# A fused attention and gated-MLP kernel on one core: x of tiles 2 and 3 loads earlier, V of three tiles is open at once, and ACT makes four more roots

## The chip, the core and the metric

The kernel runs on one NeuronCore of a Trainium2 chip. Five engines each work through their own list of instructions and wait for one another by semaphores: TensorE (PE: matrix products and transposes, written to PSUM), VectorE (DVE), ScalarE (ACT), GpSimd (POOL) and SyncE (SP), which issues all the transfers of this kernel in one queue. Weight loads of PE have a row of their own (PEld). The metric is device time in microseconds (us), less is better.

## The reference

Two branches share one layer norm over 2048 tokens of width 640: linear attention with 32 heads of width 20 and a softmax feature map, and a gated MLP of width 1536.

```python
x = A_x
xn = _layernorm(x, axis=-1)
return x + _A_ref(xn, A_wqkv, A_w_phi, A_wo) + _B_ref(xn, B_w1, B_w3, B_w2)

# _A_ref
qkv = (x @ wqkv).reshape(B, S, 3, H, Dh).transpose(2, 0, 3, 1, 4)
pq = jnp.einsum("bhsd,hdf->bhsf", q, w_phi)
pk = jnp.einsum("bhsd,hdf->bhsf", k, w_phi)
phi_q = jnp.concatenate([_softmax(pq), _softmax(-pq)], axis=-1)
phi_k = jnp.concatenate([_softmax(pk), _softmax(-pk)], axis=-1)
kv = jnp.einsum("bhsf,bhsd->bhfd", phi_k, v)
z  = jnp.einsum("bhsf->bhf", phi_k)
num = jnp.einsum("bhqf,bhfd->bhqd", phi_q, kv)
den = jnp.einsum("bhqf,bhf->bhq", phi_q, z)[..., None] + 1e-6
o = num / den          # then @ wo

# _B_ref
h = _silu(x @ w1) * (x @ w3)
out = h @ w2
```

## The kernel before

Tokens are cut into 16 tiles of 128; a column of the gated MLP's hidden layer is a unit of 128 columns by 512 tokens. The order of all instructions is written out by hand (`manual_schedule`): each engine runs its instructions in the order of the Python text, so a line moved in the text is moved in the queue of its engine, and SP's transfers go out in the order of their `ld` and `by_dma` calls. PSUM has eight banks: six come from the pool `bank`, two from `pair`. A tile taken from the pool gets a bank whose earlier tile is done with, and its first product waits for that tile's last reader.

The change lies in the first 25 us. Needed there:

- **Loads** (L163 to L178, L751, L778 to L831). `ld_tiles(t, n)` loads x of n tiles, `ld_wv(c, 1)` one row (128 of the 640 inputs) of V's weights, 160 KB each, like one tile of x. `ld_glu1` and `ld_glu` load pieces of 256 columns of w1 and w3.
- **Layer norm.** `ln_stats` (DVE, L245 and L248) makes mean and variance of a tile. For tiles 0 to 3 `ln_root` (ACT, L263) makes the standard deviation and a DVE reciprocal (L728, in `lx`) its inverse `rstd`. For the other tiles `stats` has POOL do it, with a power and a Newton step (`ln_pow`, `ln_newton`). `ln_x` (DVE, L287) normalises x in place. `BY_DMA = 4` is the bound between the two ways.
- **Transposes.** Products need x with the width on the partitions. `by_pe(dst, t)` makes five PE transposes (L305) into one bank `pst` and two ACT copies (L309) out of it. `by_dma(t)` has SP's queue transpose a tile (L751). Of normalised x (`xnT`), tiles 0, 1 and 3 go by PE and the others by DMA.
- **Raw V.** So that V of tiles 0 to 3 need not wait for the norm, it is made of x as loaded: `by_pe(xrT, t)`, then `raw_part(t, c, ps)` for the five weight rows c (two products, 360 and 280 columns, L316). `raw_scaled` (ACT, L327) multiplies with `rstd` on the way out of PSUM; the mean's share is taken off much later.
- **First gated units.** `glu_half(i, w, sc, fi, ps)` (L478) makes one half, 256 tokens, of the gate (w1) or the up product (w3): half 0 needs tiles 0 and 1, half 1 tiles 2 and 3. Eight halves make the first two units; their banks are ga, ua, gb, ub. Then follow whole units (`unit`, L461: g2, g3) and V of the other tiles (`V(4)` on, L359). A unit is finished by tanh (ACT, L472, after a table load at L813, since the roots use another table) and two DVE products (L489, L492), which free its banks. In the text `g0 = glu_done(...)` issues tanh and `g0()` the two DVE products.

Before, raw V is done in two pairs: tiles 0 and 1 row by row as the weight rows land, then tile 2, then tile 3.

Of the kernel before, what the change touches and what calls it, by code (L numbers as in the profile page):

```python
# [8 lines left out]
P = 128  # L9
# [3 lines left out]
def kernel(  # L13
# [17 lines left out]
    nc = tc.nc  # L31
    bf = mybir.dt.bfloat16
# [9 lines left out]
    HD = D // 2  # L42
    EPS = 1e-5
    SAFE = 36.0
    BY_DMA = 4
    WARM = 20
    RAW = 4

# [18 lines left out]
    def bank(name, dt=f32):  # L67
        n = 512 if dt == f32 else 1024
        return psum.tile([P, n], dt, name=name, tag="bank")
# [86 lines left out]
    with tc.manual_schedule():  # L156
# [6 lines left out]
        def ld_tiles(t, n):  # L163
            ld(
                xin[:, (t // 4) % 3, t % 4 : t % 4 + n],
                x2[t * P : (t + n) * P, :].rearrange("(t p) d -> p t d", p=P),
            )
# [4 lines left out]

        ld_tiles(0, 1)
        ld_tiles(1, 1)
        for c in range(KD):
            ld_wv(c, 1)
        ld_tiles(2, 1)
        ld_tiles(3, 1)  # L178


        ident = one.tile([P, P], bf, name="ident")
# [57 lines left out]
        def ln_stats(*ts):  # L239
            made = []  # L240
            for t in ts:
                xt = xin[:, (t // 4) % 3, t % 4, :]
                st = work.tile([P, 2, 6], f32, name="st")
                for i in range(2):
                    nc.vector.bn_stats(out=st[:, i, :], in_=xt[:, i * HD : (i + 1) * HD])  # L245
                made.append(st)
            for t, st in zip(ts, made):
                nc.vector.bn_aggr(out=mv[:, t, :], in_=st[:])  # L248
# [40 lines left out]
                op0=ALU.subtract, op1=ALU.mult,  # L289
            )  # L290

        def x_transposed(*ts):

            for t in ts:
                xn = xin[:, (t // 4) % 3, t % 4, :]
                if t >= BY_DMA:
                    nc.sync.dma_start_transpose(out=xnT[:, :, t * P : (t + 1) * P], in_=xn)
                    continue
                by_pe(xnT, t)

        def by_pe(dst, t):
            xt = xin[:, (t // 4) % 3, t % 4, :]
            ps = bank("pst", bf)
            for c in range(KD):
                nc.tensor.transpose(  # L305
                    ps[:, c * P : (c + 1) * P], xt[:, c * P : (c + 1) * P], ident[:]
                )
            for c0, c1 in ((0, 2), (2, KD)):
                nc.scalar.copy(  # L309
                    out=dst[:, c0:c1, t * P : (t + 1) * P],  # L310
                    in_=ps[:, c0 * P : c1 * P].rearrange("p (c s) -> p c s", s=P),
                )

        def raw_part(t, c, ps):
            for i, (a, b) in enumerate(((0, CH), (CH, D))):
                nc.tensor.matmul(  # L316
                    ps[i][:, 0 : b - a],
                    xrT[:, c, t * P : (t + 1) * P],
                    wv[:, c, a:b],
                    start=(c == 0),  # L320
                    stop=(c == KD - 1),
                    skip_group_check=True,
                )

        def raw_scaled(t, ps):
            for i, (a, b) in enumerate(((0, CH), (CH, D))):
                nc.scalar.activation(  # L327
                    out=v_raw[:, t, a:b], in_=ps[i][:, 0 : b - a],
                    func=AF.Identity, scale=rstd[:, t : t + 1],
                )  # L330
# [390 lines left out]
        def stats(t0, n):  # L721
            ln_stats(*range(t0, t0 + n))
            ln_pow(t0, n)
            ln_newton(t0, n)

        def lx(t0, n):
            if t0 < BY_DMA:
                nc.vector.reciprocal(out=rstd[:, t0 : t0 + n], in_=ry[:, t0 : t0 + n])  # L728
            for t in range(t0, t0 + n):
                ln_x(t)  # L730

        T = x_transposed

        def unit(banks=None):
            return glu_unit(*glu.pop(0), banks)
# [1 line left out]
        def two(name):  # L739
            both = pair(name)  # L740
            return both[:, 0], both[:, 1]
# [11 lines left out]
        def ld_glu1(w, src, f0, f1):  # L753
            ld(w[:, :, f0:f1], src[:, f0:f1].rearrange("(c p) f -> p c f", p=P))

        by_pe(xrT, 0)
        warm(4)
        ln_stats(0)
        ln_root(0)
        by_pe(xrT, 1)  # L760
        ln_stats(1)
        ln_root(1)
        vps = [two("v0"), [bank("pv"), bank("pv")]]
        lx(0, 1)
        for c in range(2):
            raw_part(0, c, vps[0])
            raw_part(1, c, vps[1])
        T(0)
        raw_part(0, 2, vps[0])
        raw_part(1, 2, vps[1])  # L770
        lx(1, 1)
        T(1)
        raw_part(0, 3, vps[0])
        raw_part(1, 3, vps[1])
        raw_part(0, 4, vps[0])
        by_pe(xrT, 2)
        raw_part(1, 4, vps[1])
        ld_glu1(w1, B_w1, 0, 256)  # L778
        nc.gpsimd.tensor_copy(out=xin[0:1, 1, 0, 0:1], in_=ry[0:1, 1:2])
        ld_tiles(4, 2)  # L780
# [1 line left out]
        ld_tiles(6, 2)  # L782
        ln_stats(2)
        ln_root(2)
        by_pe(xrT, 3)
        ln_stats(3)
        ln_root(3)
        lx(2, 1)
        by_dma(2)
        ld_glu(256, 512)  # L790
        ld_tiles(8, 2)
        ld_tiles(10, 2)
        raw_scaled(0, vps[0])
        lx(3, 1)
        raw_scaled(1, vps[1])
        ps2 = [bank("pv"), bank("pv")]
        for c in range(KD):
            raw_part(2, c, ps2)
        ps3 = [bank("pv"), bank("pv")]
        for c in range(KD):  # L800
            raw_part(3, c, ps3)
        (sc, fa), (_, fb) = glu.pop(0), glu.pop(0)
        ga, ua = two("g0")
        glu_half(0, w1, sc, fa, ga)
        T(3)
        raw_scaled(2, ps2)
        raw_scaled(3, ps3)
        gb = bank("gp")[:]
        glu_half(0, w1, sc, fb, gb)
        glu_half(0, w3, sc, fa, ua)  # L810
# [1 line left out]
        glu_half(0, w3, sc, fb, ub)  # L812
        nc.scalar.activation(out=table[:], in_=nought[:, 0:1], func=AF.Tanh)  # L813
        nc.gpsimd.tensor_mul(out=drift[:], in0=mv[:, 0:RAW, 0], in1=rstd[:, 0:RAW])
        stats(4, 2)
        stats(6, 2)
        glu_half(1, w1, sc, fa, ga)
        glu_half(1, w3, sc, fa, ua)
        glu_half(1, w1, sc, fb, gb)
        glu_half(1, w3, sc, fb, ub)  # L820
        g0 = glu_done(sc, fa, ga, ua)
        g1 = glu_done(sc, fb, gb, ub)
        lx(4, 2)
        by_dma(4)
        by_dma(5)
        ld_tiles(12, 2)
        g0()
        g2 = unit()
        lx(6, 2)
        by_dma(6)  # L830
        by_dma(7)  # L831
        ld_tiles(14, 2)
# [155 lines left out]

    with tc.If(ok == 0):
        nc.gpsimd.memset(v_one[:, :, 0], 1.0)  # L990
        for i in range(7):
            nc.gpsimd.memset(state[:, 93 * i : 93 * (i + 1)], 0.0)
        halves = [state[:, 0 : 6 * VC], state[:, 6 * VC :]]
        with tc.For_i(0, NST, 1) as t:
            cols = bass.ds(t * P, P)
            v_unit(v_one, cols)
            phi_unit(0, wkphi, "pk", exps_less_max, cols)
            acc = pair("pkv")
            kv_unit(0, v_one, acc, True, True)
            for i, half in enumerate(halves):  # L1000
                n = half.shape[1]
                nc.vector.tensor_tensor(out=half, in0=half, in1=acc[:, i, 0:n], op=ALU.add)
        kv_done(halves)
        with tc.For_i(0, NST, 1) as t:
# [36 lines left out]
```

## Time and profile before

| what | us |
|---|---|
| median of 3 runs (267.69 to 268.8) | 268.13 |
| the profiled execution, its own time | 268.32 |
| its span, first instruction to last | 266.6 |
| busy: PE | 260.7 (98%) |
| busy: DVE | 194.3 (73%) |
| busy: ACT | 114.2 (43%) |
| busy: POOL | 91.1 (34%) |

The first 24.3 us of the profiled execution, by stretch (busy us of each engine, granted PE clock, share of the 16 DMA engines):

| stretch | PE | DVE | ACT | POOL | clock | DMA |
|---|---|---|---|---|---|---|
| 0 to 4.6 | 3.68 | 1.57 | 2.15 | 3.17 | 1.00 | 0.54 |
| 4.6 to 8.5 | 3.55 | 1.69 | 2.62 | 0.18 | 1.00 | 0.83 |
| 8.5 to 12.1 | 3.60 | 3.31 | 3.12 | 0.20 | 1.00 | 1.00 |
| 12.1 to 17.2 | 4.94 | 4.05 | 4.50 | 2.74 | 1.00 | 0.88 |
| 17.2 to 24.3 | 7.04 | 6.48 | 2.84 | 1.92 | 1.00 | 1.10 |

How to read it: times inside the profile count from the span's start. A busy share says how much of a stretch an engine had an instruction under way; a product's row includes the latency of the pipeline, so rows overlap. The time of the run is longer than the span by what lies before the first and behind the last instruction. A landing is the moment at which the last of the 16 DMA engines reports its part of a transfer.

### The profile page before, as it was taken

The numbers are of one execution on the slowest core, as the hardware profiler recorded it, in microseconds if no ns is written. First come the engines' busy times: TensorE is split into PE (matmuls) and PEld (weight loads), VectorE is DVE, ScalarE is ACT, GpSimd is POOL, SyncE is SP. The second block draws the span as 40 slices with busy tenths as digits, with TensorE's granted clock in tenths as the row PEclk, the third lists the DMA queues.
The fourth block names the chain that finished last, engine by engine and source line by source line (L and its number), as shares of the span: only waits on it lengthen the run. The fifth ranks groups of instructions, "written<-read, shape, count | busy, mean of one in ns | idle before, by whom it ended". The sixth has DMA issues, their size and how long they took to land.

```text
span 266.6 us, 5010 instructions
## 1 busy us (share of the span) xinstructions
PE 260.7 (98%) x1842; PEld 152.6 (57%) x1868; DVE 194.3 (73%) x354; ACT 114.2 (43%) x348; POOL 91.1 (34%) x88
## 2 busy tenths in 40 slices
PE   8999999999999999999999999999999999999995
PEld 7766475655556555555565555555555555644563
DVE  4679984397876877799999999999699866215121
ACT  5774344746567753356766653423322240000000
POOL 5052520055544444443355333336434543000000
PEclk9999999999999999999999999999999999999999
DMA  6989756986000002500006965274765989553681
GB/s 181 259 235 197 122 115 166 332 142 113 0 2 0 1 3 6 168 2 0 2 0 164 256 120 120 62 163 98 130 140 112 163 202 157 127 124 65 183 221 55
DMA packets 83484, 31.41 MB, mean 118 GB/s; under 512 B 71935, under 2 KB 82047, under 8 KB 83456
## 3 DMA queue, kind: packets, MB, share of 16 engines
q1 hardware_dynamic: 83456, 31.05, 53.3%
q8 instruction: 16, 0.26, 0.4%
q14 instruction: 12, 0.10, 0.1%
HBM read 11.17 MB, written 2.63 MB: 52 GB/s over the span
## 4 chain that ended last, share of the span: by engine, by line
PE 92%; DMA 3%; SPq 1%; DVE 1%; issue 1%; DVEq 0%
PE up L461 18%; PE gp L461 18%; PE acc L642 15%; PE pq L359 8%; PE pk L359 8%; PE acc L600 7%; PE pv L359 6%; PE acc L647 6%; PE pr L537 2%; PE pkv L502 2%; DMA w<-in_B_w_dram 2%; DMA reg_h<-in_A_x_dram 2%; SPq L146 1%; PE pf L445 1%; DVE st L245 1%
## 5 line engine op out<-in xcount | busy, mean ns | idle before, releaser
L425 POOL TENSOR_TENSOR phi<-phi,rk 128x1320 bf16<-128x1320 bf16 x32 | 77.2, 2412 | 107.9 <-DVE rk L424 90.7
L461 PEld LDWEIGHTS <-w 128*128 128x128 bf16 x450 | 42.6, 98 | 47.3 <-DMA w<-in_B_w_dram 0.6
L422 DVE TENSOR_REDUCE sk<-phi 128x66 f32<-128x1320 bf16 x32 | 48.8, 1524 | 17.9 <-ACT phi L388 16.7
L461 PE MATMUL up<-xnT,w 128*128 128x512 bf16 x224 | 55.8, 379 | 0.2
L461 PE MATMUL gp<-xnT,w 128*128 128x512 bf16 x207 | 54.4, 378 | 1.0 <-DMA w<-in_B_w_dram 0.2
L359 PEld LDWEIGHTS <-xnT 128*128 128x128 bf16 x440 | 41.8, 98 | 18.9
L388 ACT ACTIVATE phi<-pq 128x360 bf16<-128x360 f32 (+2 forms) x96 | 24.8, 366 | 42.2 <-issue 31.8
L642 PE MATMUL acc<-reg_h,reg_v 128*128 128x512 bf16 x180 | 41.3, 379 | 0.0
L472 ACT ACTIVATE th<-gp 128x512 f32<-128x512 f32 x47 | 28.7, 612 | 26.1 <-PE gp L461 26.1
L492 DVE SCALAR_TENSOR_TENSOR reg_h<-gs,up 128x512 bf16<-128x512 bf16 x47 | 32.3, 688 | 4.8
L489 DVE SCALAR_TENSOR_TENSOR gs<-th,gp 128x512 bf16<-128x512 f32 x47 | 30.8, 654 | 3.8 <-ACT th L472 3.8
L388 ACT ACTIVATE phi<-pk 128x360 bf16<-128x360 f32 (+2 forms) x96 | 24.9, 370 | 19.4 <-PE pk L359 19.4
L642 PEld LDWEIGHTS <-reg_v 128*128 128x128 bf16 x180 | 17.4, 98 | 19.1
L359 PE MATMUL pk<-wkphi,xnT 128*128 128x360 bf16 (+1 forms) x160 | 24.3, 299 | 0.0
L359 PE MATMUL pq<-wqphi,xnT 128*128 128x360 bf16 (+1 forms) x160 | 24.3, 299 | 0.0
L424 DVE RECIPROCAL rk<-sk 128x66 f32<-128x66 f32 x32 | 18.1, 566 | 3.2
L359 PE MATMUL pv<-reg_w,xnT 128*128 128x360 bf16 x120 | 17.1, 299 | 0.0
L245 DVE BATCH_NORM_STATS2 st<-reg_h 128x6 f32<-128x320 bf16 x32 | 13.4, 479 | 4.6 <-DMA reg_h<-in_A_x_dram 4.6
L609 DVE TENSOR_TENSOR res<-acc,xr 128x320 bf16<-128x320 f32 (+2 forms) x8 | 3.7, 488 | 15.9 <-PE acc L600 10.8
L650 DVE TENSOR_TENSOR w<-acc,v_raw 128x512 bf16<-128x512 f32 x10 | 6.6, 671 | 11.5 <-issue 5.9
L558 DVE TENSOR_TENSOR o__77<-pr,den 128x360 bf16<-128x360 f32 (+1 forms) x32 | 14.2, 486 | 0.5
L374 ACT CAST reg_v<-pv 128x360 bf16<-128x360 f32 (+2 forms) x36 | 9.8, 349 | 9.8 <-PE pv L359 9.8
(92 smaller groups left out, 217.7 us busy)
## 6 DMA issues: line engine op xcount, KB each, us to landing
w<-in_B_w_dram SPq DMA_DIRECT2D x2, 1280.0 KB, 7.4
reg_h<-in_A_x_dram SPq DMA_DIRECT2D x6, 320.0 KB, 4.8
reg_v<-in_B_w_dram SPq DMA_DIRECT2D x1, 1920.0 KB, 8.6
out_dram<-w SPq DMA_DIRECT2D x6, 320.0 KB, 2.7
w<-in_B_w_dram SPq DMA_DIRECT2D x4, 320.0 KB, 4.6
reg_w<-in_A_wqkv_dram SPq DMA_DIRECT2D x5, 160.0 KB, 3.6
reg_w<-in_A_wo_dram SPq DMA_DIRECT2D x1, 800.0 KB, 7.0
reg_h<-in_A_x_dram SPq DMA_DIRECT2D x4, 160.0 KB, 4.3
```

What stands on the lines that cost most here:

```text
L245: nc.vector.bn_stats(out=st[:, i, :], in_=xt[:, i * HD : (i + 1) * HD])
L359: nc.tensor.matmul(ps[i][:, 0 : b - a], xnT[:, c, cols], w[:, c, a:b], start=(c == 0), stop=(c == KD - 1), skip_group_check=True,)
L388: nc.scalar.activation(out=dst[:, c0 : c0 + n, g, 0:k], in_=p.rearrange("p (c f) -> p c f", c=n), func=AF.Exp, scale=1.0 - 2.0 * g,)
L422: nc.vector.reduce_sum(out=sk[:], in_=rows, axis=AX.X)
L424: nc.vector.reciprocal(out=rk[:], in_=sk[:])
L425: nc.gpsimd.tensor_mul(out=rows, in0=rows, in1=rk[:, :, :, None].to_broadcast([P, 2 * NCH, 3, Dh]))
L461: nc.tensor.matmul(ps, w[:, c, fi * P : (fi + 1) * P], xnT[:, c, sc * 512 : (sc + 1) * 512], start=(c == 0), stop=(c == KD - 1),)
L472: nc.scalar.activation(out=th[:], in_=gp, func=AF.Tanh, scale=0.5)
L489: nc.vector.scalar_tensor_tensor(out=gs[:], in0=th[:], scalar=1.0, in1=gp, op0=ALU.add, op1=ALU.mult)
L492: nc.vector.scalar_tensor_tensor(out=hT[:, 4 * sc : 4 * sc + 4, fi, :], in0=gs[:].rearrange("p (t s) -> p t s", t=4), scalar=0.5, in1=up.r ...
L600: nc.tensor.matmul(ps[:, 0 : b - a], rows[j][0], rows[j][1][:, a:b], start=(j == 0), stop=(j == len(rows) - 1),)
L642: nc.tensor.matmul(acc4, w2[:, k, cols], hT[:, 4 * g : 4 * g + 4, k, :], start=(k == 0), stop=False,)
```

## The change

Six edits:

1. x of tiles 2 and 3 goes out after two rows of V's weights instead of five.
2. `by_pe` is given its bank. Two banks `pst` serve all seven sets of PE transposes in turn; before, each took a new bank from the pool.
3. Raw V of tiles 0, 1 and 2 is open at once: rows 0 and 1 of each as its x is there, then row 2 of all three, then rows 3 and 4. Tile 3 follows, in the pair that tile 0 had. Normalised x of tiles 1 and 3 is transposed behind that.
4. `raw_scaled` of tile 2 moves from ACT to DVE.
5. `BY_ROOT = 8`: `rstd` of tiles 4 to 7 is made by ACT's root and DVE's reciprocal instead of by POOL. Their statistics, roots and normalisation all stand ahead of the load of tanh's table and of the first unit's DVE products.
6. ga and ua are taken from the pool instead of from the pair. In the built program the banks fall otherwise: ga gets that of tile 2's first V half, ua a `pst` bank, gb that of tile 2's second V half; g3 gets ga's and ua's banks, V(4) gb's and ub's, V(6) both of g2's. Before, V(6) had one of g2's and one of V(4)'s.

In the branch that is run only for extreme weights a memset is cut into 19 pieces instead of 7.

```diff
-    BY_DMA = 4
+    BY_ROOT = 8
...
-        for c in range(KD):
+        for c in range(2):
             ld_wv(c, 1)
         ld_tiles(2, 1)
         ld_tiles(3, 1)
+        for c in range(2, KD):
+            ld_wv(c, 1)
...
-        def by_pe(dst, t):
+        def by_pe(dst, t, ps):
             xt = xin[:, (t // 4) % 3, t % 4, :]
-            ps = bank("pst", bf)
...
-        def raw_scaled(t, ps):
+        def raw_scaled(t, ps, by_dve=False):
             for i, (a, b) in enumerate(((0, CH), (CH, D))):
+                if by_dve:
+                    nc.vector.tensor_scalar(
+                        out=v_raw[:, t, a:b], in0=ps[i][:, 0 : b - a],
+                        scalar1=rstd[:, t : t + 1], scalar2=None, op0=ALU.mult,
+                    )
+                    continue
                 nc.scalar.activation(
...
         def lx(t0, n):
-            if t0 < BY_DMA:
+            if t0 < BY_ROOT:
                 nc.vector.reciprocal(out=rstd[:, t0 : t0 + n], in_=ry[:, t0 : t0 + n])
...
-        by_pe(xrT, 0)
+        pst = [bank("pst", bf), bank("pst", bf)]
+        by_pe(xrT, 0, pst[0])
         warm(4)
         ln_stats(0)
         ln_root(0)
-        by_pe(xrT, 1)
+        by_pe(xrT, 1, pst[1])
         ln_stats(1)
         ln_root(1)
-        vps = [two("v0"), [bank("pv"), bank("pv")]]
+        vps = [two("v0"), [bank("pv"), bank("pv")], [bank("pv"), bank("pv")]]
         lx(0, 1)
-        for c in range(2):
-            raw_part(0, c, vps[0])
-            raw_part(1, c, vps[1])
-        T(0)
-        raw_part(0, 2, vps[0])
-        raw_part(1, 2, vps[1])
+        raw_part(0, 0, vps[0])
+        raw_part(0, 1, vps[0])
+        raw_part(1, 0, vps[1])
         lx(1, 1)
-        T(1)
-        raw_part(0, 3, vps[0])
-        raw_part(1, 3, vps[1])
-        raw_part(0, 4, vps[0])
-        by_pe(xrT, 2)
-        raw_part(1, 4, vps[1])
+        by_pe(xrT, 2, pst[0])
+        raw_part(1, 1, vps[1])
+        by_pe(xnT, 0, pst[1])
         ld_glu1(w1, B_w1, 0, 256)
...
         ln_stats(2)
         ln_root(2)
-        by_pe(xrT, 3)
+        raw_part(2, 0, vps[2])
+        raw_part(2, 1, vps[2])
         ln_stats(3)
+        by_pe(xrT, 3, pst[0])
         ln_root(3)
+        for t in range(3):
+            raw_part(t, 2, vps[t])
         lx(2, 1)
         by_dma(2)
         ld_glu(256, 512)
         ld_tiles(8, 2)
         ld_tiles(10, 2)
+        lx(3, 1)
+        for t in range(3):
+            for c in (3, 4):
+                raw_part(t, c, vps[t])
         raw_scaled(0, vps[0])
-        lx(3, 1)
+        by_pe(xnT, 1, pst[1])
         raw_scaled(1, vps[1])
-        ps2 = [bank("pv"), bank("pv")]
-        for c in range(KD):
-            raw_part(2, c, ps2)
-        ps3 = [bank("pv"), bank("pv")]
+        raw_scaled(2, vps[2], True)
+        by_pe(xnT, 3, pst[0])
+        ps3 = two("pv")
         for c in range(KD):
             raw_part(3, c, ps3)
         (sc, fa), (_, fb) = glu.pop(0), glu.pop(0)
-        ga, ua = two("g0")
+        ga, ua = bank("gp")[:], bank("up")[:]
         glu_half(0, w1, sc, fa, ga)
-        T(3)
-        raw_scaled(2, ps2)
         raw_scaled(3, ps3)
+        ln_stats(4, 5)
+        ln_stats(6, 7)
+        for t in range(4, 8):
+            ln_root(t)
+        lx(4, 2)
+        lx(6, 2)
...
         nc.scalar.activation(out=table[:], in_=nought[:, 0:1], func=AF.Tanh)
         nc.gpsimd.tensor_mul(out=drift[:], in0=mv[:, 0:RAW, 0], in1=rstd[:, 0:RAW])
-        stats(4, 2)
-        stats(6, 2)
...
         g1 = glu_done(sc, fb, gb, ub)
-        lx(4, 2)
         by_dma(4)
         by_dma(5)
         ld_tiles(12, 2)
         g0()
         g2 = unit()
-        lx(6, 2)
         by_dma(6)
         by_dma(7)
```

More of the change, by code (lines that the diff above doesn't have):

```diff
@@ L290, in ln_x @@
             )
[L292 to L299, printed above, removed]
-        def by_pe(dst, t):
+        def by_pe(dst, t, ps):
             xt = xin[:, (t // 4) % 3, t % 4, :]
-            ps = bank("pst", bf)
             for c in range(KD):
@@ L730, in lx @@
                 ln_x(t)
-        T = x_transposed
         def unit(banks=None):
@@ L990 @@
         nc.gpsimd.memset(v_one[:, :, 0], 1.0)
-        for i in range(7):
-            nc.gpsimd.memset(state[:, 93 * i : 93 * (i + 1)], 0.0)
+        for i in range(19):
+            nc.gpsimd.memset(state[:, 651 * i // 19 : 651 * (i + 1) // 19], 0.0)
         halves = [state[:, 0 : 6 * VC], state[:, 6 * VC :]]
```

## The prediction

> **What bounds the kernel now.** I read first the page's slices and chain of waits, then the chain's first 30 us in order of time, then PE's, ACT's and DVE's timelines, record by record where merged lines hide a gap.
>
> ```profile
> span 266.6 us, 5010 instructions
> PE   8999999999999999999999999999999999999995
> PE 92%; DMA 3%; SPq 1%; DVE 1%; issue 1%; DVEq 0%
> ```
>
> PE is full in every slice but the first and the last, and carries 92% of the chain. DMA, SP and DVE hold it only at the start, and there the chain runs (start us, us, what):
>
> ```profile
> 4.07 4.32 DMA reg_h<-in_A_x_dram
> ...
> 10.67 0.45 DVE reg_h L287
> ...
> 11.75 0.71 SPq L751
> ...
> 12.52 4.65 DMA w<-in_B_w_dram
> 17.16 0.05 issue
> 17.21 0.39 PE gp L461
> ```
>
> x of tiles 2 and 3 is issued eighth and ninth and lands at 8.39 and 8.84. Tile 2 is normalised until 11.12, SP spends 11.14 to 12.47 on its transpose, and only then issues the second piece of w1 (columns 256:512), which lands at 17.16, while PE waits for it. PE's timeline of that stretch (start, us; in brackets the idle time):
>
> ```profile
> 8.01 0.43 PE L316 MATMUL v<-reg_w 128*128 128x360 bf16 x2 [0.18 <-DMA reg_w<-in_A_wqkv_dram]
> 8.44 0.45 PE L305 MATMUL pst<-ident,reg_h 128*128 128x128 bf16 x5
> ...
> 14.70 1.25 PE L478 MATMUL g<-xnT,w 128*128 128x256 bf16 x10
> ...
> 17.21 1.25 PE L461 MATMUL gp<-xnT,w 128*128 128x512 bf16 x4 [0.17 <-DMA w<-in_B_w_dram]
> ```
>
> A busy row counts pipeline latency, so I measure gaps from start to start: a warm 128-column product follows the last after 0.056 us, 256 columns after 0.109, a raw part (360 and 280) takes 0.272. By these, PE is idle 0.27 before 4.62, 0.31 before 5.20, 0.35 before 8.01, 0.15 before 8.44, 0.08 before 9.36, 0.15 before 14.70 (tile 2's transpose lands at 14.66) and 0.33 before 17.21: 1.64 us. After 17.21 I find no gap but steps that look like single missing records. So PE is the bound, and the change can win at most 1.64 us, 0.6%, unless it removes work.
>
> **What it removes and adds on each engine.** PE: 40 raw parts, 35 transposes and 8 gate halves before and after, so nothing. POOL: 12 small operations go, rstd of tiles 4 to 7 (2.1 us for each pair, 13.66 to 15.76); the extra memsets stand in a branch that does not run. ACT: two scalings fewer (0.9), four roots more (0.2 each, start to start). DVE: two reciprocals and tile 2's two scalings more, 360 and 280 columns from PSUM; nearest row, 486 ns, the quotient of 360 columns (L558): 0.9 us.
>
> **Step 1, the loads.** All five rows of V's weights and the four single tiles are 160 KB in packets of 1280 bytes, so I take the landing as that of the place in the queue: x2 at 6.24 (place of row 2), x3 at 7.06, rows 2, 3, 4 at 7.97, 8.39, 8.84. Everything behind keeps its place: x of tiles 6 and 7 lands at 13.98.
>
> **Step 2, PE to 12.9.** Start 4.62 as before. Tile 0 row 1 waits for row 1 (4.99): 5.04 to 5.31; tile 1 row 0 to 5.58. Then the transposes of x2 wait for 6.24: a new gap of 0.71. Then 6.29 to 6.57, tile 1 row 1 to 6.84, tile 0's normalised transposes to 7.12. Tile 2's rows need ACT's first copy; from x2's landing to that product was 0.97 before (8.39 to 9.36), so 7.20 to 7.75; x3's transposes to 8.03. Row 2 of three tiles to 8.85 (landed 7.97), six parts to 10.48, two sets of transposes to 11.04, tile 3 to 12.40, the first gate half to 12.94. Idle: 0.27 + 0.15 + 0.71 + 0.08 = 1.21. Before, the same work (V, all transposes, one gate half) ended at 12.91. So three open tiles win nothing here: the early x buys a gap in place of those at 5.20, 8.01 and 8.44. Bounds for 12.94: 12.6 (x2 0.3 early; rows 2 to 4 then bound) to 13.5 (x2 as late in its place as it was at 8.39 in its own).
>
> **Step 3, tile 2's transpose and w1.** DVE: statistics of x2 from 6.45 (behind tile 1's normalisation), ACT's root 8.28 to 8.57 behind the copies, normalised by 9.33. SP issues the transpose at 9.35 instead of 11.14, w1's piece at 10.72 instead of 12.52. But the transfers sit behind x of tiles 6 and 7 in the engines, which are full (DMA share 1.00 from 8.5 to 12.1). In the trace all 16 parts of the transpose land together at 14.51 to 14.66, after the last straggler of that x (13.98). So it lands between 13.8 and 14.66, w1 between 16.2 and 17.0. PE needs them at 12.94 + 3 x 0.545 = 14.57 and, after four more halves, at 16.75. I take both as met: the unit g2 starts at 16.75 instead of 17.21, 0.46 won. At the late end 0.2.
>
> **Step 4, what is late next.** The roots of tiles 4 to 7 stand on ACT ahead of the tanh table. Before, ACT had nothing of x6 and x7 in its way:
>
> ```profile
> 15.56 1.28 ACT L813 ACT_TABLE_LOAD   x1
> ...
> 16.96 0.58 ACT L472 ACTIVATE th<-g 128x512 f32<-128x512 f32 x1
> ```
>
> ```profile
> 14.07 1.67 DVE L245 BATCH_NORM_STATS2 st<-reg_h 128x6 f32<-128x320 bf16 x4 [0.51 <-DMA reg_h<-in_A_x_dram]
> 15.66 0.33 DVE L248 BATCH_NORM_AGGREGATE mv<-st 128x2 f32<-128x12 f32 x2
> ...
> 17.57 0.69 DVE L489 SCALAR_TENSOR_TENSOR gs<-th,g 128x512 bf16<-128x512 f32 x1 [0.92 <-ACT th L472]
> ...
> 23.57 0.69 DVE L492 SCALAR_TENSOR_TENSOR reg_h<-gs,up 128x512 bf16<-128x512 bf16 x1
> ```
>
> Tile 7's statistics end at 15.99; its root runs 16.1 to 16.41, the load can start at 16.43, 0.87 later than now. From the load to DVE's first product were 2.01 us (15.56 to 17.57): now 18.44. Before, the normalisation of 6 and 7 (18.90 to 19.61, 0.71) stood inside DVE's chain; now it runs ahead of it, in DVE's wait, so the chain up to g2's last product ends at 24.26 + 0.87 - 0.71 = 24.42.
>
> PE meets it at the PSUM banks, which the change deals anew. g3's gate takes ga's bank, free at 18.44 + 0.69 = 19.13: PE is there at 18.92, wait 0.2. V(4) takes gb's and ub's, free at 21.2: PE comes at 21.3. V(6) takes both of g2's (before, one of them and one of V(4)'s), the second free at 24.42; its second product, 0.15 in, waits, so V(6) in effect starts at 24.28. Before: 24.26. What step 3 won is given back.
>
> **Step 5, hidden.** Transposes of 4 and 5 go out 0.24 later (reciprocal 15.91, tile 4 done 16.55; 16.57 instead of 16.33), and SP's queue passes it on: of 6 and 7, at 19.8 and 21.1, though their x is ready 1.3 us sooner. Landing times as before (4.2, 3.5, 3.9, 3.2) give 20.8, 21.4, 23.7, 24.3, for V(4) at 21.3, V(5) at 22.7, V(6), V(7) at 25.6: covered, by 0.5 or so. DVE's extra 0.9 (10.65 to 11.55) ends about when x4 lands (11.37); without that cover it would be paid in the chain above.
>
> **Sum.** +0.02 us on the profiled execution, 268.32 (span 266.6 and 1.7 around it), which lies 0.19 over the median. Against the median, 268.13: **268.1**. Bounds of the steps: -0.45 (all of step 3 kept) to +0.4 (x6 and x7 0.4 later still; 13.5 in step 2 alone makes g2 start at 17.3 and adds only 0.1) give 267.7 to 268.5; the three runs themselves span 267.69 to 268.8.
>
> **Rivals.**
> *Gain kept* (0.24). x6 and x7's last part was 1.2 us behind the other fifteen (12.74), beside a fetch of 16 KB on another queue at 12.07 that took 1.04 us. Without it DVE starts their statistics when it is done with 4 and 5 (13.55): the chain is 0.5 earlier, V(6) starts near 23.85, 0.4 won: 267.7. Against it: the fetch comes with PE's progress, which is the same at 12.
> *The tanh chain later still* (0.09), the slower side. Place: ACT between root 7 and tanh. V(6) already waits, so each us there costs one, on the whole kernel. Over 0.5% from 1.34 us on; price if the load has 1.4 us to spare for emptying ACT: 269.5. Against it: at 15.56 it started 0.02 behind the last scaling and tanh followed 0.12 behind its end.
> On that the Trainium skill (ScalarE: Activation LUTs, What ACT_TABLE_LOAD costs) counts a drain of 1380 ns with every switch, beside the 1283 of the load. The rows here agree with the 1283 and show no drain after it.
> *The clock falls back* (0.03). Products step by 0.107 until 4.01 and 0.056 from 4.07. The change adds a gap of 0.71 and more transposes just behind. Half speed over some 3.4 us, as long as it took to come up, costs 1.7: 269.8. Against it: 1.1 us of gaps between 4.35 and 9.36 did nothing of the kind.
> The Trainium skill (TensorE: Matmul & The Clock Gate, Part 1 and Part 4) has the clock drop after an idle window of about 3.4 us and does not count transposes as busy; by that rule taken strictly this stretch is at risk.
> *All gaps go* (0.03): 1.64 us, 266.5. Nothing lands early enough for it.
> *The change doesn't do what it says* (0.05): the transpose lands no sooner, w1 at 17.16; g2 starts at 17.21 as before, the chain still decides V(6): 268.2.
> *Forecast*: 0.56.
>
> **How the numbers follow.** No change within 0.5% (1.34 us, about what a measurement here can tell from none) holds forecast, gain kept and no effect: 0.85. Slower: 0.09 + 0.03, less a little that ends under the bound, 0.11. Faster: 0.04. The range, 267.2 to 269.3, takes the step bounds with half a us of spread between runs, and leaves out the last three extremes.
>
> **What would show it.** x2 landing near 6.2 and a PE gap of about 0.7 before its transposes; SP's first transpose at 9.4; g2 at 16.8 with no wait for w1; the table load at 16.4 instead of 15.56; DVE's first product near 18.4; PE waits on DVE at g3 (0.2) and V(6), which starts at 24.1 to 24.3. If V(6) starts at 23.9 or sooner, the gain is kept; at 25 or later, the tanh chain or V's loads are worse than I have them.

## The result and the profile after

| | before | after |
|---|---|---|
| median of 20 runs each | 268.11 (267.49 to 268.8) | 268.81 (268.21 to 269.99) |
| profiled execution, its own time | 268.32 | 268.21 |
| its span | 266.6 | 266.5 |

The ratio is 1.0031, with a 95% interval of 1.0019 to 1.0043: the changed kernel is slower, by about 0.7 us. That is inside the range of the prediction and within the 0.5% that it called no change, but it is a real loss where a sum of nothing was forecast. Measured again later, on another chip and beside other kernels, the ratio is 1.0017 (1.0006 to 1.0027): 268.31 against 267.96. (A ratio is worked out from all the runs and can differ a little from the quotient of the medians.) Most of the section on experiments is about where these 0.35 to 0.7 us come from.

The profiled execution of the changed kernel is its fastest run, so its page shows nothing of the loss. Span, share of PE in the chain:

```profile
span 266.5 us, 5035 instructions
PE 99%; DVE 0%; issue 0%
```

PE holds 99% of the chain instead of 92%: the transfers, SP and DVE have left it. The chain of that execution in order of time (start us, us, what), around V of tiles 4 to 7:

```profile
20.36 1.08 PE up L459 x5
21.43 2.87 PE pv L357 x21
24.30 0.01 issue
24.31 2.72 PE pv L357 x19
```

V is 40 products in a row, and yet the chain cuts them behind the 21st. That is where V(6) turns from its first bank to its second. How long it waits there the pieces don't tell, but the records do: V(6)'s first product starts at 23.99 and its second at 24.31, 0.32 apart where 0.15 is usual, which is a wait of 0.17 us. The same place in the profile of the later measurement, where the run took 269.08 us and the span was 267.3:

```profile
23.28 0.56 DVE gs L487
23.84 0.03 issue
23.87 0.02 DVEq L490
23.89 0.45 issue
24.34 0.70 DVE reg_h L490
25.04 0.04 issue
25.08 2.73 PE pv L357 x19
```

Here the wait is long enough (0.73) for the chain to leave PE: V(6)'s second product starts when DVE's second product of g2 (L490, L492 before) is done, since that one reads the bank which V(6) needs. And between DVE's two products stands a piece called issue, 0.45 us, in which DVE waits for nothing that the profile of this run shows.

What comes ahead of it, in the profiled execution: ACT's timeline, then DVE's.

```profile
15.30 0.48 ACT L265 ACTIVATE ry<-mv,eps 128x1 f32<-128x1 f32 x2 [0.70 <-DVE mv L250]
15.80 1.28 ACT L815 ACT_TABLE_LOAD   x1
...
17.20 1.06 ACT L470 ACTIVATE th<-gp 128x512 f32<-128x512 f32 x2
```

```profile
17.81 0.69 DVE L487 SCALAR_TENSOR_TENSOR gs<-th,gp 128x512 bf16<-128x512 f32 x1 [0.63 <-ACT th L470]
...
22.43 0.63 DVE L487 SCALAR_TENSOR_TENSOR gs<-th,gp 128x512 bf16<-128x512 f32 x1
23.57 0.69 DVE L490 SCALAR_TENSOR_TENSOR reg_h<-gs,up 128x512 bf16<-128x512 bf16 x1 [0.51 <-DVE gs L487]
```

The table load now follows ACT's roots, and these DVE's statistics of tiles 6 and 7 (mv L250). DVE's last product of g2 starts at 23.57, exactly when it did before, although its first one is 0.40 earlier (22.43 instead of 22.83): the 0.51 in the brackets has eaten that.

PE up to there, in the same execution:

```profile
6.28 0.65 PE L297 MATMUL pst<-ident,reg_h 128*128 128x128 bf16 x5
...
7.39 0.72 PE L308 MATMUL pv<-reg_w 128*128 128x360 bf16 x4
...
12.59 1.25 PE L476 MATMUL gp<-xnT,w 128*128 128x256 bf16 x10
...
16.96 1.24 PE L459 MATMUL gp<-xnT,w 128*128 128x512 bf16 x5
```

x2's transposes start at 6.28, raw V is done at 12.59, g2 starts at 16.96, with no wait for a transfer from 7.39 on.

### The profile page after: what moved, and what is told of

The parts are those of the page before. It is cut to its first block, busy times and chain, and to the rows that moved or that the text cites. A ratio compares the mean times of both kernels' runs of the same rounds, so it can differ in the third digit from the quotient of the medians.

```text
span 266.5 us, 5035 instructions
## 1 busy us (share of the span) xinstructions
PE 262.6 (99%) x1868; PEld 153.3 (58%) x1868; DVE 195.7 (73%) x358; ACT 114.1 (43%) x350; POOL 87.5 (33%) x76
## 4 chain that ended last, share of the span: by engine, by line
PE 99%; DVE 0%; issue 0%
PE gp L459 18%; PE up L459 18%; PE acc L640 15%; PE pq L357 8%; PE pk L357 8%; PE acc L598 7%; PE pv L357 6%; PE acc L645 6%; PE pr L535 2%; PE pkv L500 2%; PE pv L308 2%; PE pf L443 1%; PE pst L297 1%; PE idle L221 1%; PE gp L476 1%; PE up L476 1%
## 5 line engine op out<-in xcount | busy, mean ns | idle before, releaser
L459 PE MATMUL gp<-xnT,w 128*128 128x512 bf16 x225 | 55.9, 379 | 0.0
L490 DVE SCALAR_TENSOR_TENSOR reg_h<-gs,up 128x512 bf16<-128x512 bf16 x48 | 33.0, 688 | 5.4 <-DVE gs L487 0.5
L487 DVE SCALAR_TENSOR_TENSOR gs<-th,gp 128x512 bf16<-128x512 f32 x48 | 31.4, 655 | 4.3 <-ACT th L470 4.3
```

The lines of the kernel that those rows point to most:

```text
L459: nc.tensor.matmul(ps, w[:, c, fi * P : (fi + 1) * P], xnT[:, c, sc * 512 : (sc + 1) * 512], start=(c == 0), stop=(c == KD - 1),)
L487: nc.vector.scalar_tensor_tensor(out=gs[:], in0=th[:], scalar=1.0, in1=gp, op0=ALU.add, op1=ALU.mult)
L490: nc.vector.scalar_tensor_tensor(out=hT[:, 4 * sc : 4 * sc + 4, fi, :], in0=gs[:].rearrange("p (t s) -> p t s", t=4), scalar=0.5, in1=up.r ...
```

## The experiments

Three theories stood at the outset for why the changed kernel is slower and why its runs differ by over a us. A: the clock's rise, which came at 6.6 us in the first profile of after instead of 3.9. B: the transfers, which land differently from run to run. C: V(6)'s wait for g2's bank at the end of the chain landing of x6 and x7, statistics, roots, table load, tanh, DVE's products (the chain theory below).

**More profiles of both kernels.** Unchanged kernels, one profile each; the last three of the seven were taken after the first of the other experiments.

> The changed kernel unchanged, for another trace. In the trace at hand (268.21 us, span 266.5, the fastest of 20 runs) PE's 128-column products step by 0.107 us until 6.7 us and by 0.056 after it; in the trace of before they do so until 4.0. The 20 runs spread over 1.8 us (268.21 to 269.99), those of before over 1.3. Theory A, the clock's rise: the moment at which PE gets to full speed falls at random, and the changed kernel has less idle time behind 6 us to absorb a late one; then a run of 269 us or more shows the rise at 7 us or later, and its first gated unit starts later by as much as its time is longer. Theory B, the transfers: a late landing (row 4 of V's weights, x of tiles 6 and 7) holds PE, and the rise of the clock is the same in slow and fast runs. Theory C, the bank wait at V(6): slow runs show V(6) waiting more than the 0.17 us of the fast one, with V's stage at the same time.

> As for the look before: theory A ties the span to the moment of PE's rise (one for one beyond about 7 us), B to a landing, C to the wait at V(6).

> As for the two looks before: theory A ties the span to the moment of PE's rise, B to a landing, C to the wait at V(6).

> The kernel before, unchanged, for a second trace. Theory A: its rise also falls at another moment than 4.0, up to 7 or so, and its span changes by at most 0.5 us, since PE waits there for weights and x anyway. Theories B and C: the rise is at 4.0 again.

> The changed kernel again, as it is, on the chip of the three others. Chain theory: ratio 1.002 to 1.004 to the kernel before, spread over 268.2 to 270, with V(6)'s second product 10.9 us behind the landing of x of tiles 6 and 7 and the end 242.20 behind that product. Rival (the difference belonged to the chip of the first runs): ratio within 0.999 to 1.001.

> The kernel before, one more profile. The step at issue is the 0.46 us that PE waited for w1 ahead of g2 (17.21) in the profiled execution that the prediction was made on; in the second profile g2 started at 16.39 without a wait. If that wait was one execution's, g2 starts at 16.4 to 16.8 here and V(6)'s second product at 23.8 to 24.0 with no wait on a bank; rival: the wait is usual, g2 at 17.0 to 17.3 with w1 behind it and V(6) at 24.3. In both, the end lies 242.20 behind V(6)'s second product.

> The kernel before once more, with the same two readings: g2 at 16.4 to 16.8 and V(6)'s second product at 23.8 to 24.0 (the wait for w1 was one execution's), or g2 at 17.0 to 17.3 and V(6) at 24.3 (it is usual); the end 242.20 behind V(6)'s second product.

Read from the records of these traces (us; the wait is the distance of V(6)'s first two products less the usual 0.152):

| profile | run | last part of x of tiles 6, 7 | table load | g2 | V(6), 1st product | wait | V(6), 2nd product | span |
|---|---|---|---|---|---|---|---|---|
| after | 268.21 | 13.35 | 15.80 | 16.96 | 23.99 | 0.17 | 24.31 | 266.50 |
| after, 2nd | 268.53 | 13.62 | 16.02 | 16.91 | 23.94 | 0.44 | 24.53 | 266.73 |
| after, 3rd | 268.30 | 13.41 | 15.82 | 16.46 | 23.49 | 0.69 | 24.33 | 266.53 |
| after, 4th | 269.39 | 14.47 | 16.88 | 17.35 | 24.51 | 0.73 | 25.39 | 267.59 |
| after, 5th | 269.08 | 14.17 | 16.57 | 17.04 | 24.20 | 0.73 | 25.08 | 267.28 |
| before | 268.32 | 13.98 | 15.56 | 17.21 | 24.25 | 0 | 24.41 | 266.61 |
| before, 2nd | 267.84 | 13.38 | 15.22 | 16.39 | 23.71 | 0 | 23.86 | 266.06 |
| before, 3rd | 268.21 | 14.21 | 15.27 | 17.12 | 24.15 | 0 | 24.30 | 266.50 |
| before, 4th | 267.82 | 12.99 | 15.56 | 16.73 | 23.76 | 0 | 23.91 | 266.11 |

Four things stand in it. In every row the span ends 242.20 us behind V(6)'s second product: nothing behind it makes a difference, so that product is the finish to look at. In the five rows of after it comes 10.91 to 10.96 behind the landing of x of tiles 6 and 7; in the rows of before that distance is anything from 10.09 to 10.92, and the table load doesn't follow the landing. The fifth profile of after belongs to the later measurement: both distances came as expected there, and the ratio, 1.0017, a little under the 1.002 to 1.004 expected. The wait, 0.55 on the mean, is in every row of after and in none of before. That it is 0.73 twice is no chance: in these two, the 4th and the 5th, g3 has waited for its bank already (0.12 and 0.13, from start to start), so that DVE's chain sets PE's arrival too. And PE comes to V(6) no earlier than before: its first product is at 24.02 on the mean of five against 23.97 on the mean of four, and g2 starts at 16.94 against 16.86.

The moment at which PE's products change from steps of 0.107 us to 0.056 differs as well: the last slow one is at 6.6, 5.6, 4.8, 3.5 and 3.8 us in the rows of after and at 3.9, 3.5, 4.0 and 5.8 in those of before. The fourth profile of after, its slowest, has the earliest rise of the five, and the profiled one, its fastest, the latest. So a late rise of the clock is not what costs; the granted clock shows nothing of it.

The wait for w1 ahead of g2 was one execution's, although the third profile has g2 as late as the rival said (17.12), for another reason. PE of the second, the third and the fourth profile of before:

```profile
16.39 1.24 PE L461 MATMUL gp<-xnT,w 128*128 128x512 bf16 x4
17.74 1.25 PE L461 MATMUL up<-xnT,w 128*128 128x512 bf16 x5
```

```profile
14.94 1.25 PE L478 MATMUL g<-xnT,w 128*128 128x256 bf16 x10 [0.52 <-DMA xnT<-reg_h]
...
17.12 1.24 PE L461 MATMUL gp<-xnT,w 128*128 128x512 bf16 x4
```

```profile
16.73 1.24 PE L461 MATMUL gp<-xnT,w 128*128 128x512 bf16 x4
```

g2 has no wait for w1 in three of four executions. The second waits 0.28 inside g2, ahead of its up product (17.74, where 17.47 was due): w3's piece landed at 17.70. The third is late at g2, but by tile 2's transpose (0.52), and that lands 0.6 to 0.7 behind x of tiles 6 and 7 in all nine rows, whether it is issued at 9.1 to 9.3 or at 10.5 to 11.1.

**Four edits of the changed kernel, and one of the kernel before.** The first four ran beside 35 runs of the kernel before (267.94), the last beside 35 others (267.96).

*One DVE instruction more*, at the start of the list, where DVE has time:

```diff
         nc.vector.memset(nought[:], 0.0)
+        pad = one.tile([P, 1], f32, name="pad")
+        nc.vector.memset(pad[:], 0.0)
```

> The changed kernel with one DVE memset of one column added near 1 us, where DVE waits for x; nothing else. In all four traces of the changed kernel the end of the run lies 242.2 us behind the second product of V(6), and that product waits for DVE's last product of unit g2, which starts 0.47 us after the wait ahead of it has ended, where every other one of its kind starts after 0.07. Theory S (this 0.41 is DVE's instruction stream, fetched at a fixed place of its list): one instruction more moves that place on to an instruction that stands and waits anyway, the 0.41 goes from the chain, and the time falls by 0.2 (fast runs, where PE itself arrives then) to 0.4 (slow ones): about 268.4 at the median against 268.8. Rival (the 0.41 belongs to the operands, a bank shared with PE): it stays, and the time too, 268.8.

*The fifth edit undone*, POOL makes `rstd` of tiles 4 to 7 again:

```diff
-    BY_ROOT = 8
+    BY_ROOT = 4
...
-        ln_stats(4, 5)
-        ln_stats(6, 7)
-        for t in range(4, 8):
-            ln_root(t)
-        lx(4, 2)
-        lx(6, 2)
...
+        stats(4, 2)
+        stats(6, 2)
...
+        lx(4, 2)
...
+        lx(6, 2)
```

> The changed kernel with edit 5 alone undone: POOL makes the inverse deviation of tiles 4 to 7, their normalisation stands where it stood before, tanh's table loads right behind tile 3's scaling. Theory S (the chain x of tiles 6 and 7, statistics, roots, table, tanh, DVE, bank of V(6) sets the end): table load near 14.3 instead of 15.8 to 16.9, DVE's last product of g2 ends 0.7 us or more sooner, V(6) no longer waits, and the time falls by 0.2 to 1.0, about 268.1 at the median, with less spread. Rival (V's new order and the loads cost the time): it stays at 268.8.

*V(6) in another bank*, everything else as in the changed kernel:

```diff
-        V(4)
+        V(4, two("pv"))
...
-        V(5, two("pv"))
+        V(5)
...
-        V(6)
+        V(6, two("pv"))
...
-        V(7, two("pv"))
+        V(7)
```

> The changed kernel with V(4) and V(6) in the pair and V(5) and V(7) in banks of the pool, the reverse of now; so V(6) takes V(4)'s banks and V(7), 1.4 us later, those of g2. Nothing else moves. Theory S: V(6) starts when PE gets there and its second product no longer waits (0.17 to 0.73 us less idle in the four traces at hand), and the time falls by that much: about 268.3 at the median, and the spread shrinks. Rival (another wait stands right behind, or the time is lost elsewhere): under 0.15 us.

*The kernel before with the fifth edit alone* (statistics, roots and normalisation of tiles 4 to 7 ahead of the table load).

> The kernel before with edit 5 alone (ACT's roots for tiles 4 to 7, ahead of tanh's table); loads, V, banks of the kernel before. Theory S: the table load moves from about 15.5 to about 16.4, but V(6) has one of g2's banks, the gate's, and one of V(4)'s, so it does not wait for g2's last product: the time is that of before within 0.2 us. Rival (the roots ahead of tanh cost the time by themselves, whatever the banks): slower than before by 0.4 or more.

*Both the second and the third*: roots undone and V(6) in another bank.

> A candidate for a kernel better than both: the changed kernel with its fifth edit undone (POOL makes rstd of tiles 4 to 7, normalisation at its old places) and V(4) and V(6) in the pair, V(5) and V(7) in banks of the pool. Chain theory: neither table load (13.8 to 14.0 instead of 15.8) nor bank can hold V(6), which then starts when PE gets there, 23.5 to 24.0 by the gaps before it; the end 242.20 behind its second product, 266.0 to 266.3: ratio 0.998 to 1.0005. Rival (V(6)'s normalised x by transposing transfer decides in its place, since tiles 6 and 7 are normalised late again): V(6) at 24.0 to 24.3 with a wait for a transfer, ratio 1.000 to 1.002, as with one of the two parts alone.

| kernel | median us | ratio to before, 95% interval | V(6), 2nd product | wait |
|---|---|---|---|---|
| one DVE instruction more | 268.20 | 1.0013 (1.0002 to 1.0024) | 24.18 | 0 |
| fifth edit undone | 268.09 | 1.0006 (0.9995 to 1.0016) | 23.88 | 0 |
| V(6) in another bank | 267.97 | 1.0006 (0.9993 to 1.0018) | 24.15 | 0 |
| before with the fifth edit | 268.26 | 1.0016 (1.0008 to 1.0025) | 24.21 | 0 |
| fifth edit undone, other bank | 267.98 | 1.0006 (0.9996 to 1.0016) | 23.80 | 0 |

Either way of taking V(6) out of the reach of DVE's chain, an earlier chain or another bank, brings the kernel to a time that can't be told from the time before; both at once bring no more, where 0.998 to 1.0005 was expected. The intervals overlap with that of the changed kernel measured again (1.0006 to 1.0027), so the times alone don't settle it; the traces show that V(6)'s wait is gone. In the trace with the fifth edit undone the table load is at 13.99 instead of 15.80 and DVE's last product of g2 at 22.44. In the one with the other bank the chain is as late as in the changed kernel (15.81; 23.58 with 0.51 idle), and PE runs its 40 products through. None of the three beats the kernel before: what the first four edits and the sixth bring is not to be seen in the times.

The DVE instruction added moved the stall. DVE's timeline of that kernel:

```profile
22.46 0.63 DVE L489 SCALAR_TENSOR_TENSOR gs<-th,gp 128x512 bf16<-128x512 f32 x1
23.20 0.69 DVE L492 SCALAR_TENSOR_TENSOR reg_h<-gs,up 128x512 bf16<-128x512 bf16 x1
```

From one product to the next are 0.74 us again, as in before, instead of 1.14. In the kernel before with the fifth edit the 0.51 stands one unit later, at g3's second product:

```profile
25.66 0.69 DVE L492 SCALAR_TENSOR_TENSOR reg_h<-gs,up 128x512 bf16<-128x512 bf16 x1 [0.51 <-PE pv L359]
```

Here, and in three of the runs below, the profile names PE's products of V as what ended the wait; but the idle time is 0.51 or 0.52 wherever PE is, so PE isn't what sets it. What the traces share is the place. In all twelve that have this idle time it stands ahead of DVE's 64th record, the sequencer's waits counted. In the eight others there is none in this stretch; but in four of these, the two with the DVE instruction and the two with the fifth edit undone, DVE stands still at its 320th record, five times 64. DVE of the kernel with one DVE instruction more:

```profile
168.81 0.69 DVE L492 SCALAR_TENSOR_TENSOR reg_h<-gs,up 128x512 bf16<-128x512 bf16 x1 [0.46 <-DVE gs L489]
```

In these four traces alone the end lies 242.30 behind V(6)'s second product instead of 242.20: PE makes one longer step (0.30) some 9 to 10 us behind that stall, which is likely its doing, though no run shows it. So the stall belongs to a place in DVE's list of instructions, not to g2 or to a wait.

The ratio of the kernel with one DVE instruction more, 1.0013, lies between: in its profile the landing is at 13.33 and V(6) doesn't wait, but a chain that is only 0.41 shorter (10.5 behind the landing) would make it wait wherever the landing is much past 13.6. That last part is argued, not shown.

The kernel before with the fifth edit alone is slower in its time (1.0016) but not in its span: over its twelve runs the span is 266.15 on the mean, against 266.23 in the runs of before beside it. What it is slower by lies ahead of the first or behind the last instruction (2.19 us outside the span instead of 1.75). So the roots ahead of the table load cost the work itself nothing where V(6) doesn't take both of g2's banks; why the time outside the span is longer in this kernel alone is not shown.

**The chain made longer by a known amount.** If V(6)'s second product is where the chain meets PE, each us added to the chain is one on the whole kernel. An ACT copy that nothing reads goes in behind the roots:

```diff
             ln_root(t)
+        late = one.tile([P, D], bf, name="late")
+        nc.scalar.copy(out=late[:], in_=wv[:, 0])
```

> The changed kernel with one ACT instruction more, a copy of 128x640 bf16 (which nothing reads) between the root of tile 7 and the load of tanh's table. ACT's copy of 128x384 columns took 0.485 us, so my estimate for this one is 0.7 to 0.8. Chain theory (V(6)'s second product waits for the bank of g2's up product, at the end of x of tiles 6 and 7 - statistics - roots - table load - tanh - DVE): the table load about 0.7 us later, DVE's first product too, V(6)'s second product near 25.0 to 25.2 instead of 24.3 in a profile with x of tiles 6 and 7 at 13.4, and the end 242.20 us behind that: 0.6 to 0.8 us on the whole kernel, a ratio to the kernel before of 1.005 to 1.006. Rival (V(6)'s wait is only what the trace shows, and what makes the changed kernel slower is elsewhere, in the clock's rise or the transfers): the wait grows but PE makes it good later or the end doesn't follow it; ratio 1.003 as without the copy.

> The same ACT copy of 128x640 bf16, but with the banks of V(4) to V(7) changed over as in the earlier run: V(6) no longer takes g2's banks, V(7) does, which begins 1.36 us later. Chain theory: the table load and DVE's products are as late as in the run with the copy alone, but V(6) doesn't wait, and V(7)'s second product, due near 25.5, meets its bank free or waits 0.1 to 0.2: ratio 1.000 to 1.002, some 0.5 us or more below the other run with the copy. Rival (the later table load costs through something else than V(6)'s bank, the transposes of tiles 4 to 7 or g3's bank): as slow as the run with the copy alone, ratio about 1.005.

The first of the two missed: 268.13, ratio 1.0014 (1.0002 to 1.0025), no slower than the changed kernel beside it (268.31). The second gave what was expected, 268.19, 1.0012 (1.0000 to 1.0025). The chain of the first, in order of time:

```profile
18.79 0.70 DVE gs L487
19.49 0.04 issue
19.53 1.24 PE gp L459 x5
20.77 1.08 PE up L459 x5
21.85 5.43 PE pv L357 x40
```

V's 40 products are in one piece, although DVE's last product of g2 ended only at 25.25, later than V(6)'s second product (24.56). The copy had made the pool deal out the banks anew: in the built program V(6)'s second bank is now that of V(4)'s first half, as it was before the change. So the experiment had taken away what it meant to lengthen, and agrees with the bank without measuring its price. What the later tanh does cost here is g3's wait for its bank, 0.75 from start to start, up to 19.53; PE still reaches V(6) at 24.40.

For the price, V(4) goes to the pair and V(5) to the pool, which leaves V(6) both of g2's banks in all four kernels below:

```diff
-        V(4)
+        V(4, two("pv"))
...
-        V(5, two("pv"))
+        V(5)
```

> The changed kernel with V(4) in the pair and V(5) in banks of the pool and no copy: the base of the three others. V(6) still takes both of g2's banks. Both theories: as the changed kernel, V(6)'s second product 10.9 behind the landing of x of tiles 6 and 7, ratio to the kernel before 1.0015 to 1.003.

> The copy of 128x640 on ACT again (0.71 us in the runs before), now with V(6) held to both of g2's banks: V(4) moves to the pair and V(5) to banks of the pool, so that the pool deals V(6) the banks it has in the changed kernel. Chain theory: V(6)'s second product comes 11.6 us behind the landing of x of tiles 6 and 7 (10.9 without the copy), at 25.0 to 25.7, the end 242.20 behind it, and the median 0.6 to 0.8 above that of the run without the copy beside it: ratio to the kernel before 1.004 to 1.006. Rival (a later tanh costs only g3's wait for its bank, about 0.6 as in the two earlier runs with the copy, and V(6)'s bank adds nothing): ratio 1.0010 to 1.002, as those two.

> As the run before it, with two such copies (1.42 us). Chain theory: V(6)'s second product 12.3 behind the landing of x of tiles 6 and 7, the median 1.3 to 1.5 above the run without a copy and 0.6 to 0.8 above that with one: one for one, ratio 1.007 to 1.009. Rival as there: g3's wait grows to about 1.3, but less than that arrives at the end; ratio at most 1.004.

> The run with one copy and V(6) in g2's banks, with one small DVE memset more at the start, which in an earlier run moved DVE's stall of 0.41 us out of the products of g2. Chain theory with that stall in the chain: V(6)'s second product 11.2 behind the landing of x of tiles 6 and 7 and the median 0.3 to 0.4 below the same kernel without the memset. Rival (the stall is elsewhere made good, or moves to another place of the same chain): median as without the memset, within 0.15.

| kernel | median us | ratio to before (267.91), 95% interval | V(6)'s 2nd product behind the landing | PE's wait there |
|---|---|---|---|---|
| no copy | 268.63 | 1.0027 (1.0015 to 1.0039) | 24.06 - 13.13 = 10.93 | 0.19 |
| one copy, 0.71 us | 269.14 | 1.0056 (1.0038 to 1.0074) | 25.00 - 13.46 = 11.54 | 0.74 |
| two copies, 1.42 us | 270.06 | 1.0088 (1.0058 to 1.0117) | 25.56 - 13.27 = 12.29 | 0.74 |
| one copy, one DVE instruction more | 268.86 | 1.0048 (1.0026 to 1.0071) | 24.95 - 13.82 = 11.13 | 0.33 |

Traces and times agree with one for one; by the times, two copies are clear of none, and the intervals of one and none just touch. One copy puts V(6)'s second product 0.6 later against the landing, two put it 1.4 later, and the medians rise by 0.5 and 1.4. Where the copies lengthen the chain, part of the price is paid early, as g3's wait for its bank (0.21 with one copy, 0.98 with two), and the rest at V(6), 0.74 in both. The end of it with two copies, from the chain:

```profile
24.82 0.70 DVE reg_h L490
25.52 0.04 issue
25.56 2.45 PE pv L357 x17
```

The DVE instruction takes 0.41 out of the same chain, 11.54 to 11.13; DVE in that trace:

```profile
23.47 0.63 DVE L489 SCALAR_TENSOR_TENSOR gs<-th,gp 128x512 bf16<-128x512 f32 x1
24.21 0.69 DVE L492 SCALAR_TENSOR_TENSOR reg_h<-gs,up 128x512 bf16<-128x512 bf16 x1
```

The medians differ by 0.28, of ten runs and six, whose intervals overlap; 0.3 is what the traces give, since 0.10 of the 0.41 is lost again later (the end lies 242.31 behind V(6)'s second product here). The share of the stall is shown by the traces rather than by the times.

## Why the prediction went wrong

**Step 1, the loads: most of them sooner than forecast.** x2 landed at 5.69 in the profiled execution and at 5.80 to 6.38 in the other four (6.24 forecast; two of the five are later than that), x3 at 6.10 to 6.83 (7.06).

**Step 2, PE to 12.9: right in its end, but set beside one execution of before.** The first gate half starts at 12.59, 12.54, 12.09, 12.22 and 12.51; forecast 12.40. So V, all transposes and one gate half end at 12.94 on the mean, as forecast. In the four executions of before the same work ended at 12.91, 12.57, 12.61 and 12.90, 12.75 on the mean, and the step had only the first. The gap of 0.71 before x2's transposes is not one of the profiled execution: its clock was still low at 6.6, and the slow products filled the time. That three open tiles win nothing here holds; on the mean they lose 0.19.

**Step 3: the transpose goes out at 9.34 as forecast (9.35) and lands at 14.00, w1 at 15.13, but the 0.46 is not won.** The step took g2's start in one execution of before, 17.21, as the usual one. The mean over four is 16.86, and after it is 16.94. Part of the reason was written down and not followed to its end: the transpose lands behind x of tiles 6 and 7 whenever it is issued. w1 lands at 15.6 on the mean against 16.3, but PE had needed that in one execution of four, and w3 earlier in another. In all, PE waits 0.24 on the mean between that gate half and V(6) after the change (g3's wait for its bank counted), against 0.37 before: 0.13 won, less than step 2 lost.

**Step 4 is the step that failed, by its size: the stretch from the landing of x of tiles 6 and 7 to V(6)'s second product.** Its mechanism is what the runs show: roots ahead of the table load, V(6) in both of g2's banks, its second product at the end of DVE's chain. From the landing of x6 and x7 (13.98) to that product it counted 10.45 (V(6) in effect at 24.28, and 0.15 to the second product: 24.43); measured are 10.91 to 10.96 in six traces (the five of after, and the kernel with its banks held and no copy). Of the 0.47 that it was short, 0.41 is DVE's stall between g2's two products. A trace of before couldn't have shown it there: that product is DVE's 59th record before, and the four instructions that the change adds, with one wait, make it the 64th. The other 0.06 is the first unit's pair of products, 0.79 from start to start instead of 0.73. With 10.92 and the mean landing of 13.80, V(6)'s second product comes at 24.72, where PE would have been there at 24.18: some 0.55 late, and with nothing won in step 3 to set against it, that is the loss. The means of the rows (24.73 after, 24.12 before) give 0.61, the times 0.35 to 0.7.

The step also left out what a dependence on a landing does to the spread. Before, the landing of x6 and x7 moved between 12.99 and 14.21 and reached PE only through tile 2's transpose and the pieces of w1 and w3; after, its last straggler goes one for one into the time, through the table load as well: 268.21 with a landing of 13.35, 269.39 with 14.47.

**Step 5: covered, as said.** No wait for a transfer stands before V(4) to V(7) in any of the traces.

**The sum.** It set 24.43 for V(6)'s second product against 24.41; the means are 24.73 and 24.12. Of the 0.59 between, 0.29 is on the side of before, whose profiled execution had a wait that most have not, and 0.30 on the side of after: 0.47 of chain too short, less 0.18 for a landing at 13.80 on the mean instead of 13.98. Told by steps, of means against means, the loss of 0.61 is 0.19 from step 2, less 0.13 from step 3, and 0.55 from step 4. The bounds of the steps ended at +0.4; only the half us of spread around them held 268.81.

**The rivals.** *Gain kept* had the condition right and the result wrong: x6 and x7 did land 0.6 sooner in the profiled execution, but PE was at V(6) at 23.99 only, and the stall put its second product to 24.31. *The tanh chain later still* priced the place rightly, one for one through V(6): two copies of 1.42 us cost 1.4. Its lateness of 1.34 us or more did not come: in the profiled execution the load starts 0.02 behind the last root and tanh 0.12 behind the load's end. The Trainium skill (ScalarE: Activation LUTs, What ACT_TABLE_LOAD costs) counts a drain of 1380 ns with every switch of tables. This trace shows none; with it the execution would have taken some 269.6 (268.21 + 1.38, an estimate from the page's figure). *The clock falls back*: no trace shows it; when the clock first rises varies from run to run, and is not tied to the time. *All gaps go* and *no effect* were not seen.

## What to carry to other kernels

A gap priced from one profiled execution may be that execution's alone: take three or four profiles before spending an edit on it, and compare means of the moment at which the full engine goes on. When an edit puts work ahead of a chain that frees PSUM banks, follow the chain from its landing to the bank's next taker and ask which unit takes it; where the pool deals the banks, look at the built program, since a change of one instruction elsewhere can deal them anew, in an experiment too. On a full engine such a wait costs one for one, and giving the bank to a unit that comes 1.4 us later takes it away.

## What the runs showed of the hardware

DVE stands still for some 0.4 us at certain places of its list of instructions: 0.51 idle between two products that otherwise are 0.10 apart. In twelve of the twenty traces the place is its 64th record, in four others (0.46 idle) its 320th, and the four of the kernel before have no such stall at either. One instruction more ahead of it takes it away from the product it was at. What DVE waits for is not shown. A transfer of 8 KB on an instruction queue starts 0.85 to 1.63 us behind the stall in the twelve traces (24.85 in the profiled execution), but also in those without it (26.19 in the profiled execution of before); that DVE waits for its next instructions is a guess.

The rise of PE's clock at the start comes anywhere from 3.5 to 6.6 us into the span in five profiles of one kernel, while the granted clock of the page shows full speed in every slice.
